# Issuing weight fetches from ScalarE and zero fills from VectorE in a fused delta-rule and SwiGLU kernel

## The chip, the cores and the metric

The kernel runs on one core of one Trainium2 chip. The metric is device time in microseconds, the median of several executions. All runs quoted here are fast: none is over 1.5% above the fastest of its kernel. Kernels are compared only within the same rounds.

## The reference, cut to what matters

```python
q, k, v: (4, 8, 768, 48) float32;  beta: (4, 8, 768);  weights: float64
k_n = k / (norm(k) + 1e-6)
for t in range(S):                       # the delta rule, one state per batch and head
    y[t]  = q[t] @ state
    state = state + beta[t] * outer(k_n[t], v[t] - k_n[t] @ state)
x = y as (3072, 384)
xn = x / rms(x) * rms_g
out = (silu(xn @ w_gate) * (xn @ w_val)) @ w_out      # 384 -> 1536 -> 384
```

The weights come as 64-bit floats. The kernel turns them into 32-bit ones with integer and float operations, tile by tile: 18 tiles of 128 x 768 elements, 768 KB each.

## The kernel before

The recurrence is done in chunks of 128 tokens. For each chunk 128 triangular blocks of 32 x 32, one per partition, are inverted together on VectorE (one long serial chain), then TensorE applies the recurrence, and the feed-forward of earlier tokens fills TensorE meanwhile. The prologue: chunk 0 and the 18 weight tiles, before the first feed-forward matmul can start. The zero fills and the fetch:

```python
def setup():
    for t in kpad + qpad:
        nc.vector.memset(t[:, :, D:DP], 0.0)
    load_k(0); load_k(1); load_q(0)          # on SP's queue
    fetch()                                  # weight tile 0
    # ... beta, more loads, fetch() of tile 1, identity, masks
    nc.gpsimd.memset(gp_all[HC:C, :, 0:HC], 0.0)
    for t in state + [tt_all]:
        nc.gpsimd.memset(t, 0.0)
    # ... small constants

def fetch():
    i = len(raws)
    if i < len(todo):
        raw = bits.tile([128, WT], I64, name="raw", bufs=3)
        src = todo[i][1]
        to = raw if len(src.shape) == 2 else raw.rearrange("p (n m) -> p n m", m=DM)
        nc.sync.dma_start(out=to, in_=src)
        raws.append(raw)
```

A tile is read by VectorE four times. `split` reads the high words twice (exponent at L228, mantissa at L238; either may come first), ScalarE does four steps, and `rest` reads the high words (sign, L257) and the low words (L265). Only after L257 and L265 is the buffer free. There are three buffers, so tile n+3 is fetched into tile n's buffer.

```python
def weights(dts):
    for i, (dst, src) in enumerate(todo):
        fetch()
        # ... from the tile after the first inversion on: issue after it
        exp = split(dst, raws[i])
        if last is not None:
            rest(*last)
        last = (dst, raws[i], exp)
        yield dts[i]
```

A batch's k is normalised in a chain over three engines: ScalarE squares (L283), VectorE sums (L285, L287), GpSimd takes the power -- a square root -- (L289), VectorE adds and inverts (L291, L292), and GpSimd multiplies (L293). The stages are generators run by a plan of nominal times, and a scheduler then fixes each engine's instruction order; so a change of queue can change every engine's order.

## Time and profile before

| | before |
|---|---|
| median (range), 4 runs | 921.6 us (920.0 to 922.9) |
| stage 1: until the inversion starts | 61.8 us |
| stage 2: inversion | 25.6 us |
| stage 3: until the first feed-forward matmul | 69.0 us |
| rest: TensorE bound (busy 745.9 us) | 764.5 us |

The table comes from cutting the trace at three events: the first step of the inversion (L372), its last (the start of `gblk`, L388), and the first `p_gv` matmul. In the stretches view of the kernel before, each row has start:end and length, then busy time and number of instructions of PE, PEld, DVE, ACT and POOL, granted clock, DMA share and GB/s:

```profile
0.00:61.76 61.76, 18.28 (x166) 14.03 (x166) 40.30 (x103) 40.29 (x74) 20.85 (x26) 0.78 0.70 183
61.76:87.36 25.60, 0.00 (x0) 0.00 (x0) 23.47 (x63) 0.00 (x0) 0.00 (x0) 0.50 0.00 0
87.36:156.34 68.98, 37.25 (x666) 34.01 (x666) 50.19 (x77) 49.92 (x74) 3.37 (x5) 0.52 0.53 151
156.34:920.80 764.46, 745.93 (x7310) 577.65 (x7310) 298.84 (x834) 202.67 (x551) 62.89 (x67) 1.00 0.17 39
```

Stage 3 is 68.98 us with VectorE busy 50.19: 18.8 us idle. The waits of VectorE in that stage say what the idle time is waiting for (total us, times, longest):

```profile
DVE u L546 <- PE p_x L534: 10.3, 2, 6.6
DVE u L541 <- PE p_z L525: 4.0, 2, 2.0
DVE state L486 <- PE p_s L476: 2.8, 2, 2.2
```

Together 17.1 us, all of it for steps of the recurrence on TensorE, none for a weight tile. The next three tiles were asked for at 103.45 us and landed at 108.64, 110.52 and 112.39, so up to 108.6 VectorE waits for a step and for a tile at once, and only one is named. After that the first tile is there, but its first read stands behind further steps of the recurrence in VectorE's order and starts at 118.95: some 8 us of the idle time are then waits for the recurrence alone.

At the start of the kernel, GpSimd's timeline (start, length, line, operation; in brackets the idle time before it and what ended it):

```profile
1.71 1.80 POOL L161 MEMSET gp<- 64x2048 f32 x1
...
5.01 1.82 POOL L163 MEMSET tt<- 128x2048 f32 x1
6.81 3.70 POOL L289 TENSOR_TENSOR knrm<-ksum,half 128x8 f32<-128x8 f32 x2
...
15.28 1.43 POOL L293 TENSOR_TENSOR kpad<-kpad,krec 128x384 f32<-128x384 f32 x1 [3.53 <-DMA nbeta<-in_beta_dram]
```

### The profile page before, as it was taken

How to read it: one execution, taken by the hardware profiler on the slowest of the kernel's cores; microseconds unless marked ns; L12 is line 12 of the kernel's file. 1: busy time of each engine (PE TensorE's matmuls, PEld its weight loads, DVE VectorE, ACT ScalarE, POOL GpSimd, SP SyncE). 2: the span in 40 equal slices, each digit the busy share in tenths (PEclk: the TensorE clock that was granted, in tenths of full speed). 3: DMA queues.
4: the chain of work that ended last, by engine and by line, in shares of the span. 5: the costliest groups of instructions: out<-in, count | busy, mean ns of one | idle time of the engine just before them, and what ended most of it. 6: DMA issues, size and time to landing. Idle time of an engine off the chain costs nothing.

```text
span 920.8 us, 19355 instructions
## 1 busy us (share of the span) xinstructions
PE 801.5 (87%) x8142; PEld 625.7 (68%) x8142; DVE 412.8 (45%) x1074; ACT 292.9 (32%) x698; POOL 87.1 (9%) x98
## 2 busy tenths in 40 slices
PE   3310773899999999999999999999999999999998
PEld 2200762677778777777677777777777777787776
DVE  5879389328424329234348143266142374221110
ACT  5741487431133431223421223321233411320101
POOL 7100001300003100013000022000021000000000
PEclk9655555999999999999999999999999999999999
DMA  8541454111312210312111322112221113000000
GB/s 200 161 131 49 136 156 119 24 35 41 79 30 63 38 43 18 82 36 62 29 45 51 57 46 56 32 37 69 41 53 34 17 41 76 8 19 1 18 1 17
DMA packets 150933, 51.77 MB, mean 56 GB/s; under 512 B 142368, under 2 KB 145440, under 8 KB 150848
## 3 DMA queue, kind: packets, MB, share of 16 engines
q1 hardware_dynamic: 150848, 50.55, 22.3%
q8 instruction: 64, 1.05, 0.5%
q14 instruction: 21, 0.17, 0.1%
HBM read 36.37 MB, written 14.16 MB: 55 GB/s over the span
## 4 chain that ended last, share of the span: by engine, by line
PE 65%; DVE 21%; ACT 4%; DMA 3%; issue 2%; POOL 1%; SPq 0%; POOLq 0%; ACTq 0%
PE p_gv L614 30%; PE p_o L601 15%; DVE tmp L372 8%; DVE ttb L381 7%; PE p_y L463 3%; PE p_z L516 2%; PE p_g L327 2%; PE p_k L498 2%; PE p_x L534 2%; PE p_y L498 2%; PE p_v L429 1%; DMA td<-ttb 1%; DVE h_f L625 1%; DMA tt<-td 1%; PE p_w L436 1%
## 5 line engine op out<-in xcount | busy, mean ns | idle before, releaser
L614 PE MATMUL p_gv<-xt,wv_sb 128*128 128x256 f32 x864 | 216.5, 385 | 0.0
L614 PE MATMUL p_gv<-xt,wg_sb 128*128 128x256 f32 x864 | 214.0, 384 | 0.5 <-DVE xt L588 0.5
L601 PE MATMUL p_o<-wo_sb,h_f 128*128 128x384 f32 x576 | 212.7, 492 | 0.4
L614 PEld LDWEIGHTS p_gv<-xt,wg_sb 128*128 128x128 f32 x864 | 161.7, 191 | 44.3 <-DVE xt L588 0.9
L625 DVE TENSOR_TENSOR h_f<-sil,p_gv 128x256 f32<-128x256 f32 x144 | 60.3, 419 | 260.0 <-ACT sil L623 259.7
L614 PEld LDWEIGHTS p_gv<-xt,wv_sb 128*128 128x128 f32 x864 | 160.7, 191 | 23.0 <-issue 1.4
L623 ACT ACTIVATE sil<-p_gv 128x256 f32<-128x256 f32 x144 | 55.1, 383 | 338.6 <-PE p_gv L614 320.9
L601 PEld LDWEIGHTS p_o<-wo_sb,h_f 128*128 128x128 f32 x576 | 104.5, 190 | 47.8 <-DVE h_f L625 4.0
L372 DVE SCALAR_TENSOR_TENSOR tmp<-gblk,nbeta,ttb 128x31 f32<-128x31 f32 (+15 forms) x186 | 74.8, 402 | 19.0 <-DMA gblk<-gd 13.2
L381 DVE TENSOR_TENSOR ttb<-ttb,tmp 128x31 f32<-128x31 f32 (+15 forms) x186 | 63.6, 342 | 5.7
L342 DVE TENSOR_TENSOR gp<-p_g,mask 64x128 f32<-64x128 f32 x192 | 45.4, 277 | 42.9 <-ACT gp L340 37.9
L429 PE MATMUL p_v<-tt,gp 32*32 32x32 f32 x768 | 21.4, 200 | 48.2 <-DMA tt<-td 48.2
L429 PEld LDWEIGHTS p_v<-tt,gp 32*32 32x32 f32 x768 | 17.7, 113 | 57.7 <-ACT exp L247 44.2
L327 PE MATMUL p_g<-kqt 64*64 64x192 f32 x768 | 41.8, 353 | 16.9 <-DVE exp L228 9.7
L327 PEld LDWEIGHTS p_g<-kqt 64*64 64x64 f32 x768 | 30.8, 143 | 27.7 <-ACT kqt L319 13.3
L577 POOL TENSOR_TENSOR rs<-ms,mhalf 128x1 f32<-128x1 f32 x24 | 13.8, 575 | 345.1 <-DVE ms L575 345.1
L289 POOL TENSOR_TENSOR knrm<-ksum,half 128x8 f32<-128x8 f32 x24 | 39.8, 1661 | 53.6 <-DVE ksum L287 53.4
L303 PE MATMUL p_t<-ident,qpad 128*128 128x128 f32 x96 | 16.8, 303 | 32.2 <-DVE state L486 15.5
L339 ACT COPY gp<-p_g 128x128 f32<-128x128 f32 x96 | 25.4, 265 | 43.9 <-PE p_g L327 42.1
L303 PEld LDWEIGHTS p_t<-ident,qpad 128*128 128x128 f32 x96 | 11.7, 154 | 38.2 <-issue 22.1
L364 POOL MEMSET ttb<- 128x1024 f32 x6 | 5.7, 951 | 322.5 <-DMA td<-ttb 268.2
L516 PEld LDWEIGHTS p_z<-v_raw,tt 64*64 64x64 f32 x768 | 27.9, 149 | 9.1 <-issue 7.2
(85 smaller groups left out, 817.3 us busy)
## 6 DMA issues: line engine op xcount, KB each, us to landing
kpad<-in_k_dram SPq DMA_DIRECT2D x24, 192.0 KB, 2.6
qpad<-in_q_dram SPq DMA_DIRECT2D x24, 192.0 KB, 3.2
raw<-in_moe_w_gate_dram SPq DMA_DIRECT2D x6, 768.0 KB, 6.7
v_raw<-in_v_dram SPq DMA_DIRECT2D x24, 192.0 KB, 3.2
raw<-in_moe_w_val_dram SPq DMA_DIRECT2D x6, 768.0 KB, 4.7
raw<-in_moe_w_out_dram SPq DMA_DIRECT2D x6, 768.0 KB, 4.4
out_dram<-o_sb SPq DMA_DIRECT2D x24, 192.0 KB, 1.9
gd<-gp SPq DMA_DIRECT2D x96, 32.0 KB, 1.8
```

The lines of the kernel that those rows point to most:

```text
L289: nc.gpsimd.tensor_tensor(out=knrm, in0=ksum, in1=half, op=ALU.pow)
L327: nc.tensor.matmul(p_gs[j // 2][par][HC * i : HC * (i + 1), j % 2, i : i + 3].rearrange("p a t -> p (a t)"), pair[d, K1 if i else K0], pai ...
L342: nc.vector.tensor_tensor(out=to[p, :, place], in0=p_g[p, :, place], in1=mask[p, i, None].to_broadcast([p.stop, 2, HC]), op=ALU.mult,)
L372: nc.vector.scalar_tensor_tensor(out=tmp, in0=gblk[:, i, None, i + 1 :].to_broadcast(shape), scalar=nbeta[:, c, i : i + 1], in1=ttb[:, 0 : ...
L381: step = nc.vector.tensor_tensor(out=to, in0=to, in1=tmp, op=ALU.add)
L429: nc.tensor.matmul(p_v[wa, h], gp[b_v][wb, h, o : o + W], tt[b_v][wb, h, W:HC], skip_group_check=True,)
L498: nc.tensor.matmul(p_o[p, 2 * j : 2 * j + 2].rearrange("p h d -> p (h d)"), kq[:, j, place], st[:, j], start=(alone or j == 0), stop=alone ...
L516: nc.tensor.matmul(p_zs[b_z][p, h], tt[b_z][p, h], r[p, h], start=(h == 0), stop=(p is lo), skip_group_check=True,)
L601: nc.tensor.matmul(p_o[i], h_f[:, i * C : (i + 1) * C], wo_sb[:, f], start=(f == 0), stop=(f == FT - 1),)
L614: nc.tensor.matmul(p_gv[:, i], w_sb[:, t, f * 128 : (f + 1) * 128], xt[:, t], start=(t == 0), stop=(t == KT - 1),)
L623: nc.scalar.activation(out=sil, in_=p_gv[:, 0], func=ACTF.Silu)
L625: nc.vector.tensor_tensor(out=h_f, in0=sil, in1=p_gv[:, 1], op=ALU.mult)
```

## The change

The intent has two parts. The weight tiles are to be asked for on a queue of their own, so that they need not stand behind the small transfers on SP's queue; and GpSimd is to be relieved of the zero fills.

```diff
-        nc.gpsimd.memset(gp_all[HC:C, :, 0:HC], 0.0)
+        nc.vector.memset(gp_all[HC:C, :, 0:HC], 0.0)
         for t in state + [tt_all]:
-            nc.gpsimd.memset(t, 0.0)
+            nc.vector.memset(t, 0.0)
 ...
-            nc.sync.dma_start(out=to, in_=src)
+            nc.scalar.dma_start(out=to, in_=src)
```

## The prediction

> **What bounds the kernel now.** I read the busy digits in 40 slices first, then a table of stretches cut where the chain of waits changes character, then the timelines of SyncE's queue and of VectorE.
>
> ```profile
> PE   3310773899999999999999999999999999999998
> DVE  5879389328424329234348143266142374221110
> PEclk9655555999999999999999999999999999999999
> ```
>
> ```profile
> core 0: us, PE busy (x) PEld busy (x) DVE busy (x) ACT busy (x) POOL busy (x), PEclk, DMA share, GB/s
> 0.00:61.76 61.76, 18.28 (x166) 14.03 (x166) 40.30 (x103) 40.29 (x74) 20.85 (x26) 0.78 0.70 183
> 61.76:87.00 25.24, 0.00 (x0) 0.00 (x0) 23.11 (x63) 0.00 (x0) 0.00 (x0) 0.50 0.00 0
> 87.00:99.00 12.00, 3.02 (x88) 2.68 (x90) 11.38 (x14) 8.11 (x11) 1.11 (x2) 0.50 0.49 130
> 99.00:118.90 19.90, 19.08 (x390) 17.84 (x388) 3.35 (x8) 7.89 (x20) 0.55 (x1) 0.50 0.52 155
> 118.90:157.20 38.30, 16.00 (x202) 14.26 (x201) 36.65 (x58) 34.77 (x45) 1.71 (x2) 0.54 0.53 151
> 157.20:173.50 16.30, 13.59 (x121) 10.54 (x120) 7.67 (x27) 6.76 (x17) 9.88 (x9) 0.88 0.11 23
> 173.50:920.80 747.30, 731.48 (x7189) 566.34 (x7189) 290.34 (x808) 195.05 (x532) 53.02 (x59) 1.00 0.17 40
> ```
>
> From 173.5 us on TensorE is busy 731.5 of 747.3 us: nothing that this change touches can shorten that. All that it touches is the prologue, up to the first feed-forward matmul at 156.3 us. Its stages: chunk 0 is prepared while six weight tiles are split (to 61.76), then the triangular inversion, a serial VectorE chain, to 87.0, then recurrence and the other twelve tiles. In 118.9 to 157.2 VectorE is busy 36.65 of 38.3 us: it bounds that stage. In 99.0 to 118.9 it is idle for 16.5 us, though nine tiles are still to come. The queue shows why:
>
> ```profile
> 102.40 0.95 SPq L403 DMA_DIRECT2D ne<-nd  x2
> 103.45 1.34 SPq L203 DMA_DIRECT2D raw<-in_moe_w_gate_dram  x3
> ```
>
> ```profile
> 98.33 0.96 DVE L268 TENSOR_TENSOR wo_sb<-wo_sb,exp 128x768 f32<-128x768 f32 x1
> 105.91 0.55 DVE L546 TENSOR_TENSOR u<-p_z,beta_t 64x384 f32<-64x384 f32 x1 [6.63 <-PE p_x L534]
> ```
>
> The next three tiles are asked for only after 24 small transfers of the inversion's result, which took SyncE from 89.67 to 103.4. This idle time is what the change is after. The tail of the prologue chain, at the other end:
>
> ```profile
> 57.02 4.71 DMA gblk<-gd
> ```
>
> [...] Here a tile costs SyncE 0.34 to 0.38 us to issue and 4.2 to 4.9 us to land once the start-up is over, so issue is indeed small; what counts is order. [...] In the trace VectorE's 128x128 fills mean 165 ns and the 64x64 one 112, about 0.8 ns per element; the start-to-start pitch is some 1.1 ns[...].
>
> **The change part by part.** I compared instruction orders too, since a scheduler places the work: they differ on all engines, but only up to the first feed-forward matmuls; after that every engine has the same instructions in the same order. So the total is (start of the feed-forward) + 764 us, where 764 is 920.5 less 156.3.
>
> Fills. GpSimd loses 1.80 (half of gp) + 1.50 (four states) + 1.82 (tt) = 5.1 us, VectorE gains 2048 + 4 x 384 + 2048 = 5632 elements per partition[...]. VectorE had idle time of 2.07 and 2.32 us there, and the small work that it did in between is short. Its first useful input now comes later anyway (below). On the path: about 0. GpSimd gets nothing for its free time, since its first job waits for VectorE.
>
> Start-up loads. ScalarE starts two weight tiles of 768 KB at about 0.8 us, beside the 192 KB loads of k and q. Weight packets are 6 KB, those of k 192 bytes[...]. I estimate k of batch 0 at 7 instead of 3.4 us, beta at 12 to 13 instead of 9.7[...]. VectorE's order now has the copy of transposed beta ahead of the first norm sum. From there: 12.9 copy, 13.4 sum, GpSimd's power 1.65, then 16.5 for the normalisation of k, against 15.28 before: +1.
>
> Rest of stage 1. A tile is 0.47 + 0.47 + 0.87 x 3 = 3.55 us of VectorE and 4 x 0.83 = 3.32 of ScalarE. With three buffers, tile n+3 is fetched after tile n's last read. In the order before, 4.6 us or more of VectorE work lay between that read and the new tile's first use. In the new order it is 0.87 + 0.87 + 0.47 = 2.2 us for tile 3, 3.1 for tile 4 and 3.9 for tile 6, against a fetch of 4.3 plus hops: stalls of about 2.5, 1.5 and 0.7. ScalarE also issues nine fetches, 9 x 0.37 = 3.3 us, and does two of tile 6's steps (1.7) ahead of the last copies of gp. On the other side, work of tiles 2 and 3 fills ScalarE's idle time of 24 to 34 us. Walking both queues by hand with these durations, the last copy of gp ends at about 59 instead of 54.1, and the read of gd (4.71 us before, beside a weight tile; I take 4) ends at 66 to 66.5. Stage 1: **+4.5 us**, with an uncertainty of about 5.
>
> Inversion: same 63 instructions, 25.3 us, nothing changed.
>
> Stage 3, counted from the end of the inversion. VectorE's work up to the second half of the first feed-forward input is some 50 us: 41.7 for the tiles left, 1.8 for gblk, 7 for the recurrence. Were it packed, the feed-forward would start at +50 instead of +69.3: a gain of 19. But here too the new order puts the first use of tiles 10 to 17 only 1.8 to 3.1 us of work after the read that frees the buffer. The loop is then: fetch 4.3 + hops 0.1, first read of the fetched tile 0.47, the two reads of an earlier tile 0.87 + 0.87 which free the next buffer = 6.6 us per tile, against 3.55 of work. By hand: tile 9 is read at +9.7, tile 12 at +21.9, tile 17 at 21.9 + 5 x 6.4 = +54 (6.4 is what my walk gives), and behind it lie 12.5 us of rest for tiles 15 to 17, u, state and the two xt: +66.3. Stage 3: 66.3 - 69.3 = **-3 us**.
>
> Sum: 0 + 4.5 - 3 = +1.5, which is 922 us.
>
> **Rivals.** (A) The fetch goes off the bottleneck and VectorE packs: stage 3 ends near +50 to +55, and the total is 906 to 911, or 902 if stage 1 is also unharmed. For it: 16.5 us of idle VectorE, removed. Against: buffers, not SyncE, then gate fetches, and that loop has 6.6 us. (B) ScalarE's queue becomes the bound: waits in it hold back copies of gp, and of the recurrence's vs, tt and x; stages 1 and 3 both stretch by 5 to 10 us, 930 to 940. For it: the order has a fetch among ScalarE's steps of every tile. Against: ScalarE's own sum in stage 3 is some 50 us of 66. (C) The weights are hidden behind TensorE in the steady stage and nothing shows: against it, the stretch 118.9 to 157.2 has TensorE waiting.
>
> **Range and chances.** Stage 1 between -2 and +9, stage 3 between -10 and +5, partly independent: total 912 to 932 for 8 in 10. Two per cent is 18.4 us; the full gain of (A) just reaches it and only with stage 1 unharmed: 0.05. The loss needs both stages at the worst of (B): 0.05. Within 2%: 0.90.
>
> **What would show it.** The chain's gblk read should end at 65 to 67 us, the inversion some 25 us later, the first feed-forward matmul at 157 to 159; from there to the end 763 to 766 us. In stage 3 first reads of weight tiles should wait for their DMA, by about 2 us each and 6 to 7 us apart. A pace near 3.6 us would make it wrong toward (A); a fetch that lands in under 3 us would do that. ScalarE waits of several us with the recurrence's copies behind them would prove (B). A steady stage that differs by over 3 us would mean that I have overlooked something.

The 0.34 to 0.38 us to issue and 4.2 to 4.9 us to land hold for most tiles, not for all: in the trace of before, the tiles from 39.96 us on took SyncE 0.34 to 0.40 us to issue and landed after 4.2 to 4.9 us, but for one at 5.55 and the three asked for together from 103.45 us on, at 5.2 to 8.0.

## The result, and the profile after

The changed kernel is correct and takes 931.4 us (927.8 to 932.4, four runs), against 921.6 of before. The ratio is 1.010, with a 95% interval of 1.0065 to 1.0134: within 2%, but clearly slower. (Ratios here are the mean time of one kernel's fast runs over that of the other's of the same rounds, so not quite the ratio of the medians.) The total lies inside the predicted range, 9 us above the predicted value.

The same cuts in the kernel after:

```profile
0.00:64.87 64.87, 20.11 (x166) 14.64 (x166) 42.07 (x109) 40.17 (x74) 16.59 (x20) 0.74 0.64 174
64.87:90.48 25.61, 0.00 (x0) 0.00 (x0) 23.48 (x64) 0.00 (x0) 0.00 (x0) 0.50 0.00 0
90.48:165.42 74.94, 36.84 (x666) 33.66 (x667) 52.42 (x78) 48.75 (x73) 3.98 (x5) 0.53 0.51 139
165.42:928.90 763.48, 743.56 (x7310) 575.98 (x7310) 297.60 (x833) 203.07 (x551) 62.99 (x67) 1.00 0.17 39
```

Stage 1 is 3.1 us longer, the inversion the same, stage 3 6.0 us longer, the rest 1.0 shorter: together 8.1, which is the difference of the two profiled spans, 928.9 and 920.8. On the page, the busy digits of after in the 40 slices:

```profile
PE   2410157899999999999999999999999999999998
DVE  5769766526624328424239234257143375221110
```

In the fifth to seventh slice (93 to 163 us) VectorE has 7, 6, 6 where it had 3, 8, 9 before. The dip is gone, as the change wanted, but so is the dense work after it: the same work is spread thinner, not finished sooner. The waits of VectorE in stage 3 of after tell why:

```profile
DVE wv_sb L238 <- DMA raw<-in_moe_w_val_dram: 5.2, 3, 2.1
DVE wo_sb L238 <- DMA raw<-in_moe_w_out_dram: 4.7, 3, 2.2
DVE wg_sb L238 <- DMA raw<-in_moe_w_gate_dram: 4.2, 2, 2.2
DVE state L486 <- PE p_s L476: 3.0, 2, 2.0
DVE u L546 <- PE p_z L516: 2.5, 3, 1.1
DVE u L541 <- PE p_z L525: 1.2, 1, 1.2
```

Waits for the recurrence fell from 17.1 to 3.0 + 2.5 + 1.2 = 6.7 us. So what the change was after shrank by 10.4 us. But waits for weight tiles rose from 0 to 5.2 + 4.7 + 4.2 = 14.1 us, in eight waits, and VectorE was busy 2.2 us more in this stretch. (Its instructions hardly took longer: 53.5 us in before and 54.2 in after if their durations are summed one by one, 0.56 of it one more step of L541. Instructions that follow each other directly overlap in the records, by 3.3 us in before and 1.8 in after, and the busy time counts an overlap once.) The sum, -10.4 + 14.1 + 2.2 = +5.9, is the +6.0 of the stage. The wait was not removed; it changed its name.

Two of the eight waits on VectorE's timeline of after (the bracket is the idle time before):

```profile
113.78 0.56 DVE L238 TENSOR_SCALAR wv_sb<-raw 128x768 uint32<-128x768 uint32 x1 [2.10 <-DMA raw<-in_moe_w_val_dram]
...
120.33 0.56 DVE L238 TENSOR_SCALAR wv_sb<-raw 128x768 uint32<-128x768 uint32 x1 [1.92 <-DMA raw<-in_moe_w_val_dram]
```

The eight waits are of 1.2 to 2.3 us, each for the fetch of the tile read next. It is not that the DMA engines are full (their share is 0.51 in this stage): the fetch was issued late, because the buffer came free late. From the first read of tile 12 (113.78) to that of tile 17 (146.56) it is 6.56 us a tile; a tile is about 3.55 us of VectorE work. The chain of what released what shows the loop (start, length, what):

```profile
136.44 4.17 DMA raw<-in_moe_w_out_dram
140.63 0.56 DVE wo_sb L238
141.19 0.88 DVE exp L257
```

A fetch lands, VectorE reads the tile, and the last read of an older tile (L257) frees the buffer for the next fetch, issued at 142.09. From 98.16 to 146.56 us the chain holds nothing but seven fetches (33.7 us) and VectorE's steps between them; the recurrence and ScalarE's work come into it only behind the first read of tile 17.

### The profile page after: what moved, and what is told of

Same layout as the page of the kernel before. It is cut to its first block, busy times and chain, and to the rows that moved or that the text cites. A ratio compares the mean times of both kernels' runs of the same rounds, so it can differ in the third digit from the quotient of the medians.

```text
span 928.9 us, 19358 instructions
## 1 busy us (share of the span) xinstructions
PE 800.5 (86%) x8142; PEld 624.3 (67%) x8142; DVE 415.6 (45%) x1080; ACT 292.0 (31%) x698; POOL 83.6 (9%) x92
## 4 chain that ended last, share of the span: by engine, by line
PE 62%; DVE 20%; DMA 8%; ACT 4%; issue 2%; POOL 1%; SPq 0%; ACTq 0%; DVEq 0%; POOLq 0%
PE p_gv L614 29%; PE p_o L601 15%; DVE tmp L372 8%; DVE ttb L381 7%; PE p_g L327 2%; PE p_y L463 2%; DMA raw<-in_moe_w_out_dram 2%; PE p_z L516 2%; PE p_k L498 2%; PE p_y L498 2%; DMA raw<-in_moe_w_val_dram 2%; DMA td<-ttb 1%; DVE h_f L625 1%; PE p_x L534 1%; PE p_t L303 1%
## 5 line engine op out<-in xcount | busy, mean ns | idle before, releaser
L372 DVE SCALAR_TENSOR_TENSOR tmp<-gblk,nbeta,ttb 128x31 f32<-128x31 f32 (+15 forms) x186 | 74.8, 402 | 14.9 <-DMA gblk<-gd 9.0
L327 PE MATMUL p_g<-kqt 64*64 64x192 f32 x768 | 42.1, 362 | 11.2 <-ACT kqt L319 11.2
L534 PE MATMUL p_x<-tt,gp 64*64 64x64 f32 x384 | 30.7, 237 | 20.6 <-ACT tt L446 20.6
L289 POOL TENSOR_TENSOR knrm<-ksum,half 128x8 f32<-128x8 f32 x24 | 40.5, 1687 | 78.3 <-DVE ksum L287 78.0
L534 PEld LDWEIGHTS p_x<-tt,gp 64*64 64x64 f32 x384 | 27.2, 149 | 23.8 <-ACT tt L446 21.0
```

What stands on the lines that cost most here:

```text
L289: nc.gpsimd.tensor_tensor(out=knrm, in0=ksum, in1=half, op=ALU.pow)
L327: nc.tensor.matmul(p_gs[j // 2][par][HC * i : HC * (i + 1), j % 2, i : i + 3].rearrange("p a t -> p (a t)"), pair[d, K1 if i else K0], pai ...
L372: nc.vector.scalar_tensor_tensor(out=tmp, in0=gblk[:, i, None, i + 1 :].to_broadcast(shape), scalar=nbeta[:, c, i : i + 1], in1=ttb[:, 0 : ...
L534: nc.tensor.matmul(p_x[lo, h], gp[b_x][hi, h, HC * K0 : HC * (K0 + 1)], tt[b_x][hi, h], skip_group_check=True,)
```

## The experiments

Twelve kernels ran. All gave correct results. This table is for orientation; times in us, stages cut as above in the profiled execution. "Late" tiles are 9 to 17, those that stage 3 fetches.

| kernel | fills | fetches | median (range) | ratio to before [95%] | stage 1 | stage 3 |
|---|---|---|---|---|---|---|
| before | GpSimd | SP | 921.6 (920.0 to 922.9) | | 61.8 | 69.0 |
| after | VectorE | ScalarE | 931.4 (927.8 to 932.4) | 1.010 [1.0065, 1.0134] | 64.9 | 74.9 |
| fills_only | VectorE | SP | 924.3 (922.4 to 925.9) | 1.0027 [1.0007, 1.0046] | 65.0 | 69.0 |
| queue_only | GpSimd | ScalarE | 929.9 (929.1 to 930.6) | 1.0088 [1.0073, 1.0103] | 61.8 | 76.4 |
| early_act | VectorE | ScalarE 0-8, SP 9-17 | 923.3 (922.3 to 925.2) | 1.0019 [0.9999, 1.0039] | 64.0 | 67.3 |
| late_act | VectorE | SP 0-8, ScalarE 9-17 | 932.1 (930.7 to 932.6) | 1.0109 [1.0094, 1.0124] | 64.7 | 74.8 |
| fills_late | VectorE, late | SP | 916.3 (913.6 to 917.1) | 0.9933 [0.9911, 0.9955] | 56.3 | 69.0 |
| fills_late_pool | GpSimd, later | SP | 918.9 (915.6 to 920.0) | 0.9968 [0.9938, 0.9997] | 56.8 | 69.4 |
| fills_late_early | VectorE, late | ScalarE 0-8, SP 9-17 | 924.1 (923.7 to 924.5) | 1.0029 [1.0014, 1.0045] | 64.8 | 67.4 |
| a_alt4 | VectorE | ScalarE, 4th buffer for some | 925.7 (924.7 to 927.5) | 1.0045 [1.0025, 1.0064] | 62.0 | 73.1 |
| q_alt4 | GpSimd | ScalarE, 4th buffer for some | 927.7 (925.8 to 930.0) | 1.0065 [1.0045, 1.0086] | 66.0 | 70.2 |
| b_alt4 | GpSimd | SP, 4th buffer for some | 922.9 (920.4 to 924.1) | 1.0009 [0.9988, 1.0029] | 62.2 | 66.9 |
| a_full4 | VectorE | ScalarE, 4 buffers | 920.5 (919.6 to 923.9) | 0.9997 [0.9972, 1.0022] | 62.6 | 69.6 |
| a_pool | VectorE | GpSimd | 910.1 (908.0 to 910.8) | 0.9874 [0.9854, 0.9893] | 59.5 | 60.9 |

In every one of them the inversion takes 25.6 us (26.2 in fills_late_early) and the first feed-forward matmul is followed by 762.8 to 765.5 us. So the two stage columns carry the whole story. They come from one profiled execution each: after and early_act fetch alike in stage 1 and differ there by 0.9 us, so differences under 1 us say nothing.

### Which part costs, and where

The first two undo one half of the change each; the next two split the fetches by time.

**fills_only**: the two `memset` lines of the change, with the fetch left on `nc.sync`.

> Fills of zeros on VectorE, all fetches on SyncE as before. My theory (the cost lies in the fetches, by stage): 920 to 924 us, at most +2 from the kernel before; the fills end near 8 us on VectorE, where it has little else to do; inversion starts within 2 us of 61.8. Rival (the fills hold up VectorE and through it the first normalisation): inversion starts 3 us or more later and the total is 924 to 930.

**queue_only**: the fetch line of the change, with the fills left on `nc.gpsimd`.

> All fetches on ScalarE, fills on GpSimd as before. My theory: as the changed kernel within 3 us, 928 to 934, with stage 3 (end of the inversion to the first feed-forward matmul) some 75 us. Rival (the fills on VectorE are to blame): 920 to 924.

**early_act** and **late_act**: the change, with its fetch line as

```diff
-            nc.scalar.dma_start(out=to, in_=src)
+            (nc.scalar if i < 9 else nc.sync).dma_start(out=to, in_=src)    # early_act
+            (nc.sync if i < 9 else nc.scalar).dma_start(out=to, in_=src)    # late_act
```

> Fetches of tiles 0 to 8 on ScalarE, 9 to 17 on SyncE, fills on VectorE. Stage 1 has the changed kernel's order, stage 3 the order of before. My theory (the stages add up; stage 1 cost 3.1 us in the traces, stage 3 6): inversion starts near 64.9, stage 3 takes 69 to 70 us, total 923 to 926. Rival (stage 1 does all of it, stage 3 only inherits it): 929 to 933.

> Fetches of tiles 0 to 8 on SyncE, 9 to 17 on ScalarE, fills on VectorE. Stage 3 has the changed kernel's order. My theory: inversion starts near 62, stage 3 takes 75 us, total 925 to 929. Rival (ScalarE's queue harms only the start-up): 920 to 923.

The late fetches make stage 3 long, whatever else is changed: 74.9, 76.4 and 74.8 us in the three kernels whose late tiles are ScalarE's (after, queue_only, late_act), 69.0, 69.0 and 67.3 in those where they are SP's. The waits of late_act in stage 3 are those of after:

```profile
DVE wo_sb L238 <- DMA raw<-in_moe_w_out_dram: 5.2, 3, 2.7
DVE wv_sb L238 <- DMA raw<-in_moe_w_val_dram: 4.9, 3, 1.9
```

The fills make stage 1 long: 65.0 and 64.9 with VectorE's fills at the start, 61.8 and 61.8 with GpSimd's, whichever engine fetches. That is +3.3 and +3.1 us for work that I had put down at 0, and the early fetches on ScalarE, for which I had put down +4.5, change nothing in these four (61.80 against 61.76, 64.87 against 65.04). This zero is a cancellation: with them the last copy of gp ends 1.5 and 1.2 us later (55.62 against 54.09, 58.74 against 57.51), and the read of `gd` behind it is 1.5 and 1.4 us shorter (3.2 against 4.7 and 4.6). In the seven kernels in which a tile is in flight during that read it takes 4.6 to 5.0 us, in the seven others 3.2 to 3.3. A later run limits the zero further. Of the four expectations, fills_only went to the rival (start 3.3 us later, 924.3 us), queue_only and early_act to my theory in the total, and late_act, at 932.1 us with the start at 64.7, missed both: its start near 62 left the fills out.

Why the fills cost: VectorE's last add of a norm in this stage (L291, batch 0 of the next chunk) runs at 33.96 us in before, 37.37 in fills_only and, in the run fills_late that follows below, at 28.46. From there to the inversion it is 27.7 to 27.9 us in all three. So the difference arises before it. In the stretches view up to this add, for before, fills_only and fills_late:

```profile
0.00:33.96 33.96, 13.26 (x122) 10.38 (x126) 20.48 (x62) 18.00 (x37) 19.87 (x25) 0.90 0.83 207
0.00:37.37 37.37, 15.12 (x129) 11.46 (x130) 24.02 (x69) 18.31 (x37) 15.02 (x19) 0.86 0.75 188
0.00:28.46 28.46, 12.15 (x99) 9.08 (x103) 20.00 (x64) 17.93 (x36) 14.31 (x19) 1.00 0.86 212
```

VectorE (third pair) is busy 3.5 us more in fills_only than in before, which is the 5.1 us of fills less 1.6 us by which its other records come out shorter, and idle for 13.4 us against 13.5: the fills swallowed no idle time in sum. They did fill gaps (waits for the first squares fell from 2.4 us to 0, for the first tile from 2.3 to 0.4), but they hold VectorE until 7.9 us (gp at 2.37, state at 4.26, tt at 6.24), so that the first power starts at 11.56 instead of 6.81, and VectorE's waits for powers in the stage rise from 4.6 to 7.9 us: the first two batches, which it did not wait for in before, now cost 1.1 and 1.6. With ScalarE's fetches it is the same: in queue_only VectorE is busy 39.0 us of stage 1 and idle 22.8, in after 42.1 and 22.8.

### Whose relief helps: fills away from the start

**fills_late**: fetches on SP; half of gp filled by VectorE in the setup; states and tt filled by VectorE at a place where it is waiting anyway.

```diff
-        nc.gpsimd.memset(gp_all[HC:C, :, 0:HC], 0.0)
-        for t in state + [tt_all]:
-            nc.gpsimd.memset(t, 0.0)
+        nc.vector.memset(gp_all[HC:C, :, 0:HC], 0.0)
 ... # in invert(), chunk 0; masked[B - 1] is the last masked copy of batch 3
+            with tc.issue_after(masked[B - 1]):
+                for z in state + [tt_all]:
+                    nc.vector.memset(z, 0.0)
```

> The fills run alone cost 3.3 us in stage 1. Here the four states and tt (3.4 us of fills) are placed on VectorE after the last masked copy of batch 3, where VectorE waits some 5 us for the read of gd; only gp's fill (1.8 us) stays in the start-up. My theory (the cost is that fills in the start-up push the norm sums of batches 2 and 3 behind weight work, and the power on GpSimd is then waited for): inversion starts at 61.5 to 62.8, total 920 to 923. Rival (fills on VectorE cost their own time wherever they stand): inversion starts near 65, 923 to 926.

Stage 1 falls to 56.3 us and the total to 916.3. It came out better than either side had it (61.5 to 62.8, or near 65). GpSimd's start in fills_late, to be held against that of before (its kernel has these lines two higher up, so L287 and L291 are L289 and L293 of before):

```profile
5.05 3.28 POOL L287 TENSOR_TENSOR knrm<-ksum,half 128x8 f32<-128x8 f32 x2 [3.39 <-DVE ksum L285]
10.26 0.97 POOL L291 TENSOR_TENSOR kpad<-kpad,krec 128x384 f32<-128x384 f32 x1 [1.92 <-DVE krec L290]
```

Now the power has a bracket: it waits for its input, not behind fills, and starts 1.8 us earlier. The normalisation follows 5.0 us earlier than before (10.26 against 15.28): the power comes earlier, and VectorE's order has less weight work between it and the inverse. VectorE's waits for the power in stage 1 are 1.4 us in all, and its idle time up to the last add is 8.5 us instead of 13.5. The fills at 50.9 and 52.9 us fall into VectorE's wait for the read of `gd`.

**fills_late_pool**: as fills_late, but the late fills are `nc.gpsimd.memset`. The order puts them behind the first two powers, ahead of the first two normalisations.

> Fetches on SP. Only half of gp is filled by VectorE at the start; states and tt are filled by GpSimd, but the order places them behind the first two power instructions of GpSimd (states ahead of the first normalisation of k, tt ahead of the second), so 3.3 us of fills stay on GpSimd, only later. My theory (what matters is that GpSimd's first power no longer stands behind 5.1 us of fills): first normalisation of k at 10 to 12 us (15.28 in the kernel before, 10.26 with late fills on VectorE), the inversion starts at 56 to 59, the total is 915 to 919. Rival (it was VectorE, freed at the start, and its order that gained): the inversion starts above 60 and the total is 919 to 923.

Stage 1 is 56.8 us, the total 918.9: my theory's numbers. So it need not be VectorE that does the fills, nor need they be very late: they must not stand ahead of the first powers. "Relieve GpSimd" was a right aim of the change; giving the fills to VectorE at the same place lost the gain and 3 us more.

**fills_late_early**: fills_late, with tiles 0 to 8 fetched by ScalarE.

> Late fills on VectorE as in the run that beat both kernels, and the first nine tiles fetched by ScalarE, the last nine by SP. If the parts add (early fetches on ScalarE cost nothing, late fills gain 5): inversion start 55 to 58, stage 3 67 to 69, total 915 to 918. Rival, from the order, in which the first tiles are read 2.0 to 4.2 us of VectorE work after their buffer comes free instead of 7 to 13, and ahead of the norm sums: start 59 to 63, total 919 to 924.

The parts do not add: stage 1 is 64.8 us, 8.5 more than in fills_late, and the rival's side of the expectation came (924.1 us against the 919 to 924 it gave; the start is later than its 59 to 63). So "early fetches on ScalarE cost nothing" holds only where fills stand at the start, on either engine. In this order the first tiles are read 2.0 to 4.2 us of VectorE work after their buffers come free (7 to 13 in fills_late), and stage 1 shows waits of 2.4 and 2.6 us for tiles whose buffer came free late; k of batch 0 is squared at 7.8 us, as two weight tiles are fetched beside it, where it is 3.5 in before. The mechanism that I predicted for stage 1, tiles that are waited for because their buffers come free late, exists, then; in the changed kernel it stands beside the fills, and both together cost no more than one. (The late fills themselves are no longer free here: the read of `gd` landed at 64.05, and it was VectorE's order, with fills and one more norm ahead of the inversion, that held the start until 64.76.)

### Is it the buffers, or ScalarE's queue?

Two explanations are left for stage 3. Buffers: the order that comes with ScalarE's fetches reads a tile only 1.8 to 3.1 us of VectorE work after its buffer was freed (tiles 10 to 17; 4.7 to 8.6 in before), so that each fetch is waited for. Queue: a fetch that waits for its buffer on ScalarE holds back the steps of the recurrence behind it. Both are in the trace of after. A sign of the second on ScalarE:

```profile
142.52 0.59 ACT L551 ACTIVATE x<-p_x 64x512 f32<-64x512 f32 x1 [1.76 <-DVE exp L257]
...
150.81 0.58 ACT L578 ACTIVATE y<-p_y,rs 128x384 f32<-128x384 f32 x1 [3.93 <-POOL rs L577]
```

The copy of `x` belongs to the recurrence and has nothing to do with `exp`, but the fetch just ahead of it (142.09) waited for the last read of an old tile; the matmuls for `x` had ended at 141.81, so it was held for 0.7 us. And `y` waited 3.93 us for `rs`, GpSimd for `ms`, and `ms` (148.77 on VectorE) stands behind the first read of tile 17, which waited for its fetch. Three kernels added a fourth buffer for some of the tiles: tiles 3, 7 and 11 are fetched into a part of `wo_sb` that is not yet in use.

```diff
-            raw = bits.tile([128, WT], I64, name="raw", bufs=3)
+            if i % 4 == 3 and i < 12:
+                raw = wo_sb[:, 6:10].rearrange("p n m -> p (n m)").bitcast(I64)
+            else:
+                raw = bits.tile([128, WT], I64, name="raw", bufs=3)
```

**a_alt4** has it in the changed kernel, **q_alt4** in queue_only, **b_alt4** in before.

> The changed kernel with a fourth buffer for tiles 3, 7 and 11, laid in weight space that is filled last; so tiles 4 to 14 are fetched one tile earlier, 15 to 17 not. TensorE's and GpSimd's orders are the same as the changed kernel's, VectorE's nearly. My theory (the buffer loop of 6.5 us a tile): the waits of VectorE for DMA before tiles 10 to 14, 9.5 us in the trace, fall below 3; the first feed-forward matmul comes 5 to 9 us earlier than 165.4; total 922 to 927. Rival (recurrence steps held behind weight steps in ScalarE's and VectorE's queues set the pace, the DMA waits only fill time that is lost anyway): under 2 us gained, 929 to 933.

> As the run before this in its buffers, but fills on GpSimd. My theory: 3 us under that run, 919 to 924, so about the kernel before. Rival: 927 to 930, as with three buffers.

> The kernel before with the same fourth buffer. My theory: fetches 9 to 11 still wait behind the 24 small transfers on SyncE, and VectorE is then bound by its work of 3.55 us a tile, so 918 to 922. Rival (buffers limit this kernel too): under 917.

These were half a miss. In a_alt4 the total came as expected and the first feed-forward matmul 4.7 us earlier, but only 1.9 us of that in stage 3, where waits for tiles were still 9.4 us: 4.3 before tiles 10 to 14 (under 3 expected), and 5.2 for tiles 15 to 17, for which the fourth buffer is gone again. In q_alt4 stage 3 gained 6.2 us, and stage 1, whose order had changed too, lost 4.2, so the total (927.7) is the rival's. b_alt4 stayed as before in its total (922.9, just over the range), though its stage 3 is 2.1 us shorter: a further buffer gives something there too. A better test has four buffers throughout.

**a_full4**: the changed kernel with four raw buffers; the room comes from single buffers elsewhere, which only the feed-forward uses.

```diff
-            raw = bits.tile([128, WT], I64, name="raw", bufs=3)
+            raw = bits.tile([128, WT], I64, name="raw", bufs=4)
 # and xt 3 -> 2, h_f 3 -> 2, sil 2 -> 1, o_sb 2 -> 1 buffers
```

> The changed kernel with four raw buffers for all tiles (room made by one buffer less for xt, h_f, sil and o_sb, which may cost something behind the first feed-forward matmul: read the prologue alone). By the order a late tile is first read 3.2 to 6.5 us of VectorE work after its buffer comes free, against 1.8 to 3.1 with three buffers. Buffer theory (the 6.6 us loop of fetch and reads makes stage 3 long): DVE waits for raw tiles fall from 14 us to under 4, and stage 3 from 74.9 to 65 to 69. Rival (fetches in ScalarE's queue hold back the recurrence, whatever the buffers): stage 3 stays at 72 to 76 though the waits for tiles fall.

In a_full4, the remaining waits of VectorE for tiles in stage 3:

```profile
DVE wv_sb L238 <- DMA raw<-in_moe_w_val_dram: 3.3, 2, 2.0
DVE wg_sb L238 <- DMA raw<-in_moe_w_gate_dram: 1.9, 1, 1.9
```

The waits fall from 14.1 to 5.2 us and stage 3 from 74.9 to 69.6, with all fetches still on ScalarE; the total is that of before. Expected were under 4 and 65 to 69, so it is a little short, and the rival's 72 to 76 is excluded. Buffers that come free late are the cause: one more takes away 5.3 of the 6.0 us. It does not follow that ScalarE's queue is innocent, for the fourth buffer changed the queue too: ScalarE's waits behind L257 in stage 3, 11.7 us in after, are gone as well in a_full4. What separates the two is the chain of after, which up to tile 17 runs through fetches and VectorE alone; how much of the rest is due to steps held in ScalarE's queue was not measured. (The instruction order changed with the buffers, which also gave 2.2 us in stage 1, so the share is not exact. No run changed the queue and kept the order.) (The feed-forward is not hurt by the buffers taken from it: 764.3 us to the end.)

### A queue that nothing else needs

**a_pool**: the changed kernel with the fetches on GpSimd, fills on VectorE at the start.

```diff
-            nc.scalar.dma_start(out=to, in_=src)
+            nc.gpsimd.dma_start(out=to, in_=src)
```

> The changed kernel with all fetches issued by GpSimd, which has little else to do in stage 3; fills at the start on VectorE. By the order a late tile is read 4.4 to 6.4 us of work after its buffer comes free. If the loss of stage 3 is due to ScalarE's queue, as holder of the recurrence or through the order that goes with it: stage 3 is 66 to 70. If it comes from taking fetches off SP, whichever engine gets them: 73 to 77. Stage 1: at least the 3.3 us of the fills over the kernel before, inversion start at 64 to 68, later if GpSimd's fetches hold back its powers.

This was meant as a test and became the best kernel of all: 910.1 us, 1.3% under before and, by the medians, 2.3% under after. Its stage 3 and the waits of VectorE for tiles in it:

```profile
85.05:145.92 60.87, 36.41 (x666) 33.63 (x667) 51.87 (x78) 49.25 (x74) 9.30 (x14) 0.51 0.62 171
```

```profile
DVE wg_sb L238 <- DMA raw<-in_moe_w_gate_dram: 1.0, 2, 0.6
DVE wo_sb L238 <- DMA raw<-in_moe_w_out_dram: 0.5, 1, 0.5
DVE wv_sb L238 <- DMA raw<-in_moe_w_val_dram: 0.2, 1, 0.2
```

VectorE is busy 51.87 of 60.87 us; it waits 1.7 us for tiles and 4.1 + 1.0 us for the recurrence. So both sorts of wait are gone, with three buffers. The fetch itself is not faster: it holds GpSimd's sequencer for 0.53 to 0.87 us where it took ScalarE 0.33 to 0.39, and a late tile lands after 4.5, 5.2 and 6.3 us (lowest, median, highest) against 4.2, 4.5 and 6.0 in after. What differs is who waits. GpSimd stands idle for 30.5 us in stage 3 ahead of its nine fetches, waiting for buffers, and nobody waits for it meanwhile (the last fetch goes out at 123.8 us; the first `ms` for which it computes `rs` comes at 127.74); and in the order that comes with it a late tile is read 4.4 to 6.4 us of VectorE work after its buffer comes free, instead of 1.8 to 3.1. Both changed at once, so how much each of the two gives is open. Both rivals of this expectation were too pessimistic: 66 to 70 at best was expected, 60.9 came. Stage 1 is 59.5 us with the fills still on VectorE, less than the 64 expected at least; I have no experiment that explains it. Late fills together with GpSimd's fetches were not run.

## Why the prediction was right or wrong

The prediction was right in its total and its class, and wrong in the way its total came about: its terms 0 + 4.5 - 3 measured +3.1 for the first two together (taking back the fills alone undoes all of it, taking back the early fetches alone nothing) and +6.0 for the third.

- **What bounds**: right, but for one reading. The idle 16.5 us of VectorE in 99 to 118.9 us were put down to late fetches; some 8 of them came after the first of these tiles had landed (108.64). From the first feed-forward matmul to the end it was 763.5 us (predicted 764, "763 to 766"), and all of the difference lies ahead of it.
- **Fills, "on the path: about 0"**: the failed step. They cost +3.3 us (fills_only against before) and +3.1 (after against queue_only). At the pitch of 1.1 ns that the prediction read from the small fills, 5632 elements are an estimated 6.2 us, and VectorE was filling from 2.4 to 7.9 us, busy for 5.1 of it. "Its first useful input now comes later anyway" is true of the changed order, where the fills end at 8.0 us and the copy of beta starts at 13.27 (12.9 predicted). But without the fills the order is another: in queue_only VectorE reads the first tile at 5.09. And "GpSimd gets nothing for its free time" missed what the timeline of before shows, a power that starts without any wait right behind the fills: free of them it starts 1.8 us earlier, and in fills_late the inversion starts 5.45 us earlier.
- **Start-up loads and stage 1, +4.5**: measured +3.1, and the walk was good: k of batch 0 was squared at 6.2 us (3.5 before; arrival at 7 predicted, an estimate), beta landed at 12.28 (9.64 before; 12 to 13 estimated), the last copy of gp ended at 58.74 (about 59 predicted), and VectorE waited for tiles by 1.6, 1.0 and 1.2 us (2.5, 1.5 and 0.7). The mis-sized term is the read of `gd`: 3.2 us where 4 was taken. The parts were put down to the wrong half of the change, though: with the fills on GpSimd the same fetches cost 0.0 (queue_only), with the fills out of the way 8.5 (fills_late_early).
- **Inversion, unchanged**: right, 25.6 us in both.
- **Stage 3, -3**: measured +6.0. The loop of 6.6 us per tile was right (6.56 measured), with its waits of about 2 us; tile 17 was read at +56.1 us where +54 was predicted. The term that was mis-sized is the tail, "behind it lie 12.5 us of rest": it took 18.9 us from that read (146.56) to the first feed-forward matmul (165.42). The tail was added up as VectorE's own work, but of the 18.9 us VectorE was busy 13.7 and idle 5.2: the recurrence's steps were still open, each a hand-over between engines, and VectorE's order held `ms` behind the first read of tile 17, for which ScalarE's `y` then waited 3.93 us.
- **Rivals**: (A), VectorE packs, was refuted for ScalarE's queue but is close to what GpSimd's did: 910.1 us, inside the 906 to 911 named for it, though by gaining 8 in stage 3 and 2 in stage 1 rather than 14 to 19 in stage 3. (B), ScalarE's queue as the bound, came out in time (930 to 940 named, 931.4 measured), but not by its mechanism: its waits of 1.7 to 3 us are in the trace, and ScalarE's own steps are not in the chain before tile 17; a_full4 shows that most of the loss goes with one more buffer while the fetches stay on ScalarE. The stages did not both stretch by 5 to 10 us either. (C) was refuted.
- **Chances**: 0.90 for "within 2%" was fair. The centre was 9 us low, and that the total lies inside the range, by 0.6 us, was partly luck: +6.0 in stage 3 lies outside that stage's own range (-10 to +5), and the first feed-forward matmul came at 165.4, not at 157 to 159; stage 1 (1.4 us below its estimate) and the last stage (1.0 us shorter) made up for some of it.

## What to carry to other kernels

Idle time with one releaser's name may hide a second wait behind it: freeing the fetches took 10 us from the waits for the recurrence and gave 14 to waits for buffers, so ask what would gate the work next, and count buffers against the fetch time before moving a queue. Put fetches that have to wait for buffers on an engine that has nothing else to do: with the fills on VectorE in all three, the same fetches took 931.4 us from ScalarE, 924.3 from SP and 910.1 from GpSimd, though GpSimd's were the slower ones to issue (0.53 to 0.87 us against ScalarE's 0.33 to 0.39) and to land (5.2 us against 4.5); waits for tiles in stage 3 were 14.1 us with ScalarE's queue and 1.7 with GpSimd's, how much of it by the queue and how much by the order that goes with it being open. Put work that fills idle time where it stands ahead of nobody's input, even small fills at the start of the shortest queue: moved away from the start, all but gp's, they gained 5.45 us of stage 1 (fills_late), while at the same place on the other engine they cost 3.3 (fills_only). The engine itself made little difference: 2048 fp32 elements per partition took 1.80 to 1.82 us to fill on GpSimd and 1.76 on VectorE. When two parts of a change are estimated apart, test whether they run beside each other before adding them.
